# A gated-attention kernel's load phase: where extra V rows go, where row norms run, and in which order the output weights load

## The chip, the cores and the metric

The kernel runs on one core of one Trainium2 chip. The metric is the device time of one execution in microseconds (us). Before the change the median of three runs is 871.95 us (871.49 to 874.51). The engines are named as in the profile: PE (TensorE, matmul) with PEld (its weight loads), DVE (VectorE), ACT (ScalarE), POOL (GpSimd) and SP (SyncE, which here only issues DMAs).

## The reference, cut to what matters

Two blocks in sequence, in bf16. Block A is a recurrent attention: the 2048 rows are cut into 64 segments of 32; each segment is preceded by 8 memory rows, and the first 8 output rows of a segment are the memory of the next. Block B is a gated MLP with a spatial mixing matrix.

```python
for s in range(n_seg):                     # 64 segments, one after the other
    h = concatenate([mem, xs])             # 8 + 32 rows, D = 512
    q, k, v = h @ Wq, h @ Wk, h @ Wv       # 32 heads of 128
    p = softmax(mask(q @ k.T * scale))
    o = (p @ v) @ Wo
    mem = o[:8]; outs.append(o[8:])
h  = x + A(layernorm(x)); h2 = h + B(layernorm(h))
```

The weights Wq, Wk, Wv and Wo are 4 MB each.

## The kernel before

All instructions are put out by one Python function, `fast_path`, in an order written by hand; an `Emitter` derives the semaphore waits from tokens that each operation reads and writes. On each engine the instructions run in the order in which they are emitted. There is no planner; DMAs are issued by SP in order (function `sp`), and a few by ACT and POOL.

**Tiling of block A.** A segment has 40 rows: 8 of memory and 32 of x. The first 24 rows of x and the memory make up a tile of 32 columns (`hT`), which is worked on segment by segment. The last 8 rows of each segment, the "extra rows", do not depend on the memory; they are worked on for 16 segments at once (a chunk, 16 x 8 = 128 rows, `hTe`). Chunk `ck` gives queries and keys of the extra rows (`qkx_mm`, L410, into `QTx` in SBUF) and values (`vx_mm`, L429). One call of `qkx_mm` or `vx_mm` fills one PSUM bank with 16 matmuls; it is called a group here. A chunk has 16 Q/K groups and 8 V groups (`n` from 0 to 7: half `b = n // 4`, quarter `c = n % 4`).

The V groups come out with a row per extra row and 4 heads in a line, and attention wants 8 extra rows of one segment times 16 groups of heads on the partitions. So `vx_evac` copies a group to SBUF (L441, L443) and stores it to the DRAM tensor `vext_d` (L449), and `load_vx(s)` reads the rows of segment `s` back into `Vx` (L457). For chunk 0 the evacuated groups lie in `part`; the store is split: the rows of segments 0 and 1 go first, on the queue of ACT or POOL, the other rows on SP's.

**The load phase.** SP issues two tiles of x, Wq in four quarters, three tiles of x, the initial memory, then Wk, Wv and Wo in four quarters each (Wo by heads 0 to 7, 8 to 15 and so on). Meanwhile:

- Rows of x are normalized in place (`ln_inplace` = `ln_stats`, L357 and L358 on DVE, L359 and L361 on POOL, then `ln_apply`, L367 on DVE) and transposed by PE (`xT`, L375). Tiles 0 and 1 are the extra rows of chunks 0 and 1 and are normalized and transposed first; tiles 4, 5 and 6 are normalized in one stretch after the eighth step of the loop below.
- The constants for mask, sums and selections (`late_consts`) are made on POOL right behind these three norms.
- A loop of 16 steps works through the 16 Q/K groups of chunk 0 and, in each second step, one of chunk 1. `start_group` gives each group the next of four PSUM banks (`ebank`) and evacuates it on ACT and DVE in turn (L419, L421).

**A segment** (loop over `s`): Q and K (`QK`, L480), scores (`S_half`, L518 and L524), V (`V_half`, L571), sums (L539, L544), P times V (`PV_half`, L588; L594 for the extra rows, which reads `Vx`), the output projection (`Wo`, L621, in two halves of the columns, heads in the quarters 0, 2, 1, 3), its evacuation (`part_evac`, L636, L638) and the new memory rows (`mem_out`, L645, copied by L650), which the next segment's Q and K wait for. Into the gaps go groups of later chunks: one whole group per segment (`gx`, bank `XB`) and "atoms" of four matmuls (`gv`, `pour`, bank `VXB`). Segment 0 also does the eight V groups of chunk 0 (`start_v`) and two Q/K groups of chunk 1, between its own steps.

Block B follows after the last segment.

## Time and profile before

| | |
|---|---|
| median of 3 runs | 871.95 us (871.49 to 874.51) |
| the profiled execution | 872.18 us, span 870.4 us |
| PE busy | 846.9 us, 97% of the span, 20941 matmuls |
| DVE busy | 527.5 us, 61% |
| ACT busy | 420.9 us, 48% |
| POOL busy | 161.6 us, 19% |
| DMA | 76.29 MB; 20.48 MB of them in the first 85 us |
| mean granted TensorE clock | 0.995 of full speed |

The span is what the profile covers from the first to the last instruction; the execution's own time is 1.8 us longer. A line of the timeline gives the start, the length, the engine, the source line, the operation, output and inputs, and in square brackets the idle time of the engine before it and who ended that. A matmul that is pipelined behind another is shown with its drain, so lengths of neighbours overlap a little. A tile is named as in the program with f_ in front. Line numbers (L410) are those of the kernel before.

### The profile page before, as it was taken

The numbers are of one execution on the slowest core, as the hardware profiler recorded it, in microseconds if no ns is written. First come the engines' busy times: TensorE is split into PE (matmuls) and PEld (weight loads), VectorE is DVE, ScalarE is ACT, GpSimd is POOL, SyncE is SP. The second block draws the span as 40 slices with busy tenths as digits, with TensorE's granted clock in tenths as the row PEclk, the third lists the DMA queues.
The fourth block names the chain that finished last, engine by engine and source line by source line (L and its number), as shares of the span: only waits on it lengthen the run. The fifth ranks groups of instructions, "written<-read, shape, count | busy, mean of one in ns | idle before, by whom it ended". The sixth has DMA issues, their size and how long they took to land.

```text
span 870.4 us, 45576 instructions
## 1 busy us (share of the span) xinstructions
PE 846.9 (97%) x20941; PEld 474.5 (55%) x20941; DVE 527.5 (61%) x1192; ACT 420.9 (48%) x1083; POOL 161.6 (19%) x408
## 2 busy tenths in 40 slices
PE   6889999999999999999999999999999999999997
PEld 6645555555555655555565655455555544444443
DVE  3456667666666666666666666566666558363443
ACT  2345555555555555555555555455655566400000
POOL 1421212111211211121212121212211114100000
PEclk9999999999999999999999999999999999999999
DMA  9962223122230310211212121423322299132101
GB/s 324 377 189 63 65 55 65 44 61 65 61 56 26 86 46 25 73 46 53 61 42 53 46 61 43 108 67 89 70 68 62 61 224 337 35 104 91 50 13 38
DMA packets 109207, 76.29 MB, mean 88 GB/s; under 512 B 64104, under 2 KB 94512, under 8 KB 109008
## 3 DMA queue, kind: packets, MB, share of 16 engines
q1 hardware_dynamic: 108496, 73.04, 29.9%
q8 instruction: 166, 2.72, 1.3%
q14 instruction: 33, 0.27, 0.1%
q0 software_dynamic: 192, 0.20, 0.1%
q10 hardware_dynamic: 320, 0.07, 0.0%
HBM read 41.75 MB, written 20.91 MB: 72 GB/s over the span
## 4 chain that ended last, share of the span: by engine, by line
PE 95%; DVE 1%; DMA 1%; issue 1%; ACT 1%; POOL 1%; DVEq 0%; POOLq 0%
PE f_ps L480 26%; PE f_ps L621 15%; PE f_ps L571 12%; PE f_ps L1098 11%; PE f_ps L410 7%; PE f_ps L672 4%; PE f_ps L429 3%; PE f_ps L1091 3%; PE f_ps L1192 3%; PE f_ps L588 2%; PE f_ps L518 2%; PE f_ps L731 2%; PE f_ps L539 1%; PE f_ps L594 1%; PE f_ps L645 1%; PE f_ps L1059 1%
## 5 line engine op out<-in xcount | busy, mean ns | idle before, releaser
L480 PE MATMUL f_ps<-f_arena,f_hT 128*32 128x512 bf16 x4096 | 240.4, 380 | 0.1
L487 ACT ACTIVATE f_Tst<-f_ps 128x512 bf16<-128x512 f32 x256 | 145.9, 596 | 77.5 <-PE f_ps L480 77.5
L480 PEld LDWEIGHTS f_ps<-f_arena,f_hT 128*32 128x32 bf16 x4096 | 93.0, 96 | 103.4 <-ACT f_hT L650 32.7
L621 PE MATMUL f_ps<-f_arena,f_cT 128*32 128x256 bf16 x4096 | 130.8, 275 | 3.6 <-ACT f_cT L607 2.2
L571 PE MATMUL f_ps<-f_arena,f_hT 128*32 128x512 bf16 x2048 | 132.8, 378 | 0.0
L621 PEld LDWEIGHTS f_ps<-f_arena,f_cT 128*32 128x32 bf16 x4096 | 99.2, 97 | 36.7 <-ACT f_cT L607 31.6
L493 DVE STREAM_TRANSPOSE f_QT<-f_Tst 128x256 uint32<-128x256 uint32 x128 | 57.1, 446 | 82.2 <-ACT f_Tst L487 82.2
L580 DVE CAST f_V_sb<-f_ps 128x512 bf16<-128x512 f32 x128 | 88.4, 691 | 29.5 <-PE f_ps L571 29.5
L1098 PE MATMUL f_ps<-f_arena 128*128 128x512 bf16 x448 | 99.6, 379 | 0.1
L503 POOL COPY f_QT<-f_arena 128x256 bf16<-128x256 bf16 x64 | 30.6, 478 | 296.9 <-PE f_ps L524 296.9
L607 ACT ACTIVATE f_cT<-f_ps 128x320 bf16<-128x320 f32 x128 | 49.0, 434 | 59.2 <-PE f_ps L594 59.2
L609 DVE TENSOR_SCALAR f_cT<-f_ps 128x320 bf16<-128x320 f32 x128 | 56.9, 487 | 31.3 <-PE f_ps L594 31.3
L1098 PEld LDWEIGHTS f_ps<-f_arena 128*128 128x128 bf16 x448 | 43.7, 98 | 53.0 <-issue 0.6
L410 PE MATMUL f_ps<-f_hTe,f_arena 128*128 128x128 bf16 x1024 | 67.9, 225 | 3.8 <-DVE f_arena L421 3.2
L638 DVE CAST f_part<-f_ps 128x256 bf16<-128x256 f32 x64 | 27.2, 425 | 69.0 <-PE f_ps L621 69.0
L410 PEld LDWEIGHTS f_ps<-f_hTe,f_arena 128*128 128x128 bf16 x1024 | 60.3, 101 | 13.2 <-issue 8.5
L496 DVE STREAM_TRANSPOSE f_KT<-f_Tst 128x256 uint32<-128x256 uint32 x128 | 55.4, 433 | 8.1
L571 PEld LDWEIGHTS f_ps<-f_arena,f_hT 128*32 128x32 bf16 x2048 | 44.5, 95 | 28.9 <-issue 0.4
L551 ACT ACTIVATE f_R_sb<-f_ps 128x160 f32<-128x160 f32 x128 | 39.0, 305 | 42.6 <-PE f_ps L544 42.6
L1104 DVE TENSOR_TENSOR f_arena<-f_ps,f_arena 128x512 f32<-128x512 f32 x28 | 19.3, 690 | 60.7 <-PE f_ps L1098 60.7
L650 ACT ACTIVATE f_hT<-f_ps 128x16 bf16<-128x16 f32 x126 | 23.2, 184 | 55.8 <-PE f_ps L645 55.3
L636 ACT ACTIVATE f_part<-f_ps 128x256 bf16<-128x256 f32 x64 | 24.6, 384 | 46.5 <-PE f_ps L621 46.5
(113 smaller groups left out, 1123.1 us busy)
## 6 DMA issues: line engine op xcount, KB each, us to landing
wT_d<-f_wst SPq DMA_DIRECT2D x32, 256.0 KB, 2.2
f_arena<-wT_d SPq DMA_DIRECT2D x32, 256.0 KB, 5.2
f_arena<-in_A_Wq_dram SPq DMA_DIRECT2D x4, 1024.0 KB, 8.7
f_arena<-in_A_Wk_dram SPq DMA_DIRECT2D x4, 1024.0 KB, 14.0
f_arena<-in_A_Wv_dram SPq DMA_DIRECT2D x4, 1024.0 KB, 14.6
f_arena<-in_A_Wo_dram SPq DMA_DIRECT2D x4, 1024.0 KB, 13.6
f_Vx<-vext_d SPq DMA_DIRECT2D x62, 64.0 KB, 2.7
vext_d<-f_Vs SPq DMA_DIRECT2D x24, 128.0 KB, 2.1
```

Of the source, the lines that this page charges most:

```text
L410: pe(lambda e, h=h, dc=dc, hh=hh: e.matmul(ps[:, bank, hh * 128:(hh + 1) * 128], lhsT=ws[:, dc, h * DH:(h + 1) * DH], rhs=hTe[:, ck % 3, d ...
L480: pe(lambda e, dc=dc, c=c, rhs=rhs: e.matmul(ps[32 * c:32 * c + 32, bank, :], lhsT=hT[:, sl, dc, :], rhs=rhs, start=(dc == 0), stop=(dc == ...
L487: act(lambda e: e.activation(out=Tst[:, tb, :].rearrange("p (hp i r) -> p hp i r", i=32, r=2), in_=ps[:, bank, :].rearrange("p (hp r i) -> ...
L493: dve(lambda e: e.transpose(out=dst, in_=src), reads=[("T", tb)], writes=[("QT", b)])
L496: dve(lambda e: e.transpose(out=dst, in_=src), reads=[("T", tb)], writes=[("KT", b)])
L551: act(lambda e: e.activation(out=R_sb[:, b, :], in_=ps[:, bank, 224:384], func=ACT.Ln, scale=LNS), reads=[PB(bank)], writes=[("R", b)])
L571: pe(lambda e, dc=dc, c=c, c0=c0: e.matmul(ps[32 * c:32 * c + 32, bank, :], lhsT=hT[:, sl, dc, :], rhs=w_v[:, dc, c0:c0 + 512], start=(dc ...
L580: dve(lambda e: e.tensor_copy(out=V_sb[:, b, :], in_=ps[:, bank, :]), reads=[PB(bank)], writes=[("V", b)])
L607: act(lambda e: e.activation(out=dst, in_=src, func=ACT.Copy, scale=UNSC), reads=[PB(PVB[c])], writes=[("cT", c)])
L609: dve(lambda e: e.tensor_scalar(out=dst, in0=src, scalar1=UNSC, scalar2=None, op0=ALU.mult), reads=[PB(PVB[c])], writes=[("cT", c)])
L621: pe(lambda e, h=h, g=g, i=i, b=b, c=c: e.matmul(ps[32 * g:32 * g + 32, bank, 0:d1 - d0], lhsT=cTh[:, i, 8:40], rhs=w_o[:, h, d0:d1], star ...
L1098: pe(lambda e: e.matmul(ps[:, bank, 0:TB], lhsT=z2[:, sc, fb * 128:(fb + 1) * 128], rhs=wTb[tb % 2][:, :, sc, :], start=(n == 0), stop=(n ...
```

## The change

Four things change, all around the load phase and the first segments.

1. **Extra V rows.** `vext_d` gets another layout, so that a group's store writes 1 KB rows (4 heads in a line) instead of rows of 256 bytes; the load of a segment's rows reads pieces of 256 bytes instead of 512. Stores are not split any more and all go through SP. Segment 0's `Vx` doesn't go through DRAM: `vx_first` picks its 8 rows out of the eight evacuated groups by 32 matmuls with a shifted identity (`Z_sb`, made on POOL by two more operations) and one evacuation on ACT. Group 0 of chunk 0 lies in `xo` instead of `part`, as `part` slot 0 is written at the end of segment 0.
2. **Norms and constants.** `late_consts` is emitted right after the first two norms. Tile 1 is transposed after two groups. Tiles 4, 5 and 6 get their statistics and their application in the steps 6 to 9 of the loop, a piece per step.
3. **Wo.** It is loaded in eight pieces, in the order in which `Wo` uses the quarters (0, 2, 1, 3). Segment 0 does the first three quarters for both column halves before the last quarter.
4. **Order in segment 0.** V groups 2 and 3 follow the scores of the second half, 4 to 7 follow the sums; three banks instead of four are in turn. V group 0 of chunk 1 stands in four pieces around the output projection. No atoms are poured in segment 0, two instead of one in segments 1 to 3; over the whole kernel their number is the same, so that one atom fewer is left for segment 44.

```diff
@@ -235,6 +235,7 @@
     ones = sb("ones", [128, 128], BF)
     onesrc = sb("onesrc", [128, 160], BF)
     G_sb = sb("G_sb", [128, M], BF)
+    Z_sb = sb("Z_sb", [128, 56], BF)
     F_sb = sb("F_sb", [128, 32], BF)
     Sc = sb("Sc", [128, 128], BF)
     m0 = sb("m0", [M, D], BF)
...
-    vext_d = nc.dram_tensor("vext_d", [NCK, 16, 128, 2 * DH], BF, kind="Internal").ap()
+    vext_d = nc.dram_tensor("vext_d", [NCK, 128, 2, 16, DH], BF, kind="Internal").ap()
     xn2_d = nc.dram_tensor("xn2_d", [RB, 128, D], BF, kind="Internal").ap()
     h_d = nc.dram_tensor("h_d", [RB, 128, D], BF, kind="Internal").ap()
     NP = 10
@@ -317,10 +318,13 @@
     pool(lambda e: e.affine_select(out=ident[:], in_=onesrc[:, 0:128], pattern=[[-1, 128]], compare_op=ALU.is_equal,
                                    fill=0.0, base=0, channel_multiplier=1), reads=["onesrc"], writes=["ident"])
     pool(lambda e: e.memset(mhalf[:], -0.5), writes=["mhalf"])
-    em.mark_const("ident", "mhalf", "mask", "ones", "G", "F", "Sc", "bsp")
+    em.mark_const("ident", "mhalf", "mask", "ones", "G", "F", "Sc", "bsp", "Z")
 
     def late_consts():
         pool(lambda e: e.memset(ones[:], 0.0), writes=["ones"])
+        pool(lambda e: e.affine_select(out=Z_sb[:, :], in_=onesrc[:, 0:56], pattern=[[-1, 56]], compare_op=ALU.is_equal,
+                                       fill=0.0, base=24, channel_multiplier=1), reads=["onesrc"], writes=["Z"])
+        pool(lambda e: e.memset(Z_sb[:, 32:56], 0.0), writes=["Z"])
         pool(lambda e: e.memset(Sc[:], 0.0), writes=["Sc"])
         pool(lambda e: e.memset(mask[:], 0.0), writes=["mask"])
         for c in range(4):
@@ -430,9 +434,9 @@
                                                        start=(dc == 0), stop=(dc == DC - 1), tile_position=(0, 32 * c)),
                    reads=[("hTe", ck % 3), ("W", 2, n // 2)], writes=[PB(bank)])
 
-    def vx_evac(ck, n, bank, eng="act", queue="sp"):
+    def vx_evac(ck, n, bank, eng="act"):
         if ck == 0:
-            t, tok = part[:, n, :], [("part", n, 0), ("part", n, 1)]
+            t, tok = vx_home(n)
         else:
             j = vcnt[0] % 2
             vcnt[0] += 1
@@ -442,20 +446,31 @@
         else:
             dve(lambda e: e.tensor_copy(out=t, in_=ps[:, bank, :]), reads=[PB(bank)], writes=tok)
         b, c = n // 4, n % 4
-        dst = vext_d[ck, 4 * c:4 * c + 4, :, b * DH:(b + 1) * DH].rearrange("g t e -> t g e")
-
-        for k, (i0, i1) in enumerate(((0, 2), (2, CK)) if ck == 0 else ((0, CK),)):
-            r = slice(8 * i0, 8 * i1)
-            em.add("sp" if k else queue, lambda e, r=r: e.dma_start(dst[r], t[r].rearrange("p (g e) -> p g e", g=4)), dma=True,
-                   reads=tok, writes=[("vext", ck, n, k)])
+        sp(lambda e: e.dma_start(vext_d[ck, :, b, 4 * c:4 * c + 4, :], t.rearrange("p (g e) -> p g e", g=4)),
+           reads=tok, writes=[("vext", ck, n)])
 
     vcnt = [0]
 
-    def load_vx(s, queue="sp"):
+    def vx_home(n):
+        return (part[:, n, :], [("part", n, 0), ("part", n, 1)]) if n else (xo[:, 0, :], [("xo", 0)])
+
+    def vx_first(bank):
+        for g in range(4):
+            for b in range(2):
+                for c in range(4):
+                    t, tok = vx_home(4 * b + c)
+                    pe(lambda e, g=g, b=b, c=c, t=t: e.matmul(
+                        ps[32 * c:32 * c + 32, bank, b * DH:(b + 1) * DH], lhsT=Z_sb[:, 24 - 8 * g:56 - 8 * g], rhs=t[:, g * DH:(g + 1) * DH],
+                        start=(g == 0), stop=(g == 3), skip_group_check=True, tile_position=(0, 32 * c)),
+                        reads=tok + ["Z"], writes=[PB(bank)])
+        act(lambda e: e.activation(out=Vx[:, 0, :, :].rearrange("p b e -> p (b e)"), in_=ps[:, bank, 0:2 * DH], func=ACT.Copy),
+            reads=[PB(bank)], writes=[("Vx", 0)])
+
+    def load_vx(s):
         i = s % CK
-        assert all(("vext", s // CK, n, 0) in em.last_w for n in range(8))
-        em.add(queue, lambda e: e.dma_start(Vx[:, s % NVX, :, :], vext_d[s // CK, :, 8 * i:8 * i + 8, :]), dma=True,
-               reads=[("vext", s // CK, n, k) for n in range(8) for k in range(2 if 2 <= s < CK else 1)], writes=[("Vx", s % NVX)])
+        assert all(("vext", s // CK, n) in em.last_w for n in range(8))
+        sp(lambda e: e.dma_start(Vx[:, s % NVX, :, :], vext_d[s // CK, 8 * i:8 * i + 8, :, :, :].rearrange("t b g e -> g t b e")),
+           reads=[("vext", s // CK, n) for n in range(8)], writes=[("Vx", s % NVX)])
 
 
     QKB = {(0, 0): 0, (0, 1): 1, (1, 0): 6, (1, 1): 7}
@@ -621,7 +636,7 @@
                 pe(lambda e, h=h, g=g, i=i, b=b, c=c: e.matmul(
                     ps[32 * g:32 * g + 32, bank, 0:d1 - d0], lhsT=cTh[:, i, 8:40], rhs=w_o[:, h, d0:d1], start=(c == 0 and b == 0),
                     stop=(c == 3 and b == 1), tile_position=(0, 32 * g)),
-                    reads=[("cT", c), ("Wo", h // 8)], writes=[PB(bank)])
+                    reads=[("cT", c), ("Wo", b, c)], writes=[PB(bank)])
 
     def cTx_copy(s):
         j = s % 4
@@ -671,7 +686,7 @@
             h = 16 * b + 4 * qr + g
             pe(lambda e, h=h, g=g, i=8 * qr + bg: e.matmul(ps[32 * g:32 * g + 32, WXB, :], lhsT=cTx[:, rb % 2, i, :], rhs=w_o[:, h, :],
                                                            start=(i < 4), stop=(i >= H - 4), tile_position=(0, 32 * g)),
-               reads=[("cTx", rb % 2), ("Wo", h // 8)], writes=[PB(WXB)])
+               reads=[("cTx", rb % 2), ("Wo", b, qr)], writes=[PB(WXB)])
 
     def WoX_evac(rb):
         act(lambda e: e.activation(out=partx[:], in_=ps[:, WXB, :], func=ACT.Copy), reads=[PB(WXB)], writes=["partx"])
@@ -755,7 +770,7 @@
     def pour():
         if s > 3 * CK and not gv.atoms and zx and s + 2 < NSEG:
             z2_atoms()
-        return gv.pour(1)
+        return gv.pour(2 if 0 < s < 4 else 0 if s == 0 else 1)
 
     NWT = S // 64
 
@@ -767,23 +782,21 @@
     act(lambda e: e.preload_act_table_set("natural_log_exp_and_others"))
     for j in range(2):
         ln_inplace(j)
-        xT(j, 6 + j)
-        xe_copy(j, 6 + j)
+    late_consts()
+    xT(0, 6)
+    xe_copy(0, 6)
     for hq in range(4):
         load_w(1, hq)
-    ebank = (2, 3, 4, 5)
+    ebank = [2, 3, 4, 5]
     scnt = [0]
 
     def start_group(mm, ev, *a):
         cnt = scnt[0]
         scnt[0] += 1
-        bk = ebank[cnt % 4]
+        bk = ebank[cnt % len(ebank)]
         mm(*a, bk)
         eng = "act" if cnt % 2 == 0 else "dve"
-        if mm is vx_mm:
-            ev(*a, bk, eng, {"act": "act", "dve": "pool"}[eng])
-        else:
-            ev(*a, bk, eng)
+        ev(*a, bk, eng)
 
     def start_x(ck, i):
         start_group(qkx_mm, qkx_evac, ck, i)
@@ -793,12 +806,15 @@
 
     for i in range(16):
         start_x(0, i)
+        if i == 1:
+            xT(1, 7)
+            xe_copy(1, 7)
         if i % 2 == 1:
             start_x(1, i // 2)
-        if i == 7:
-            for j in range(4, 7):
-                ln_inplace(j)
-            late_consts()
+        if 7 <= i < 10:
+            ln_apply(i - 3)
+        if 6 <= i < 9:
+            ln_stats(i - 2)
         if i == 10:
             xT(4, 6)
             ring_copy(0, 6)
@@ -812,9 +828,11 @@
     for hq in range(4):
         load_w(2, hq)
     wor = A_Wo.rearrange("h e d -> e h d")
-    for hq in range(4):
-        sp(lambda e, hq=hq: e.dma_start(w_o[:, 8 * hq:8 * hq + 8, :], wor[:, 8 * hq:8 * hq + 8, :]), writes=[("Wo", hq)])
-        em.mark_const(("Wo", hq))
+    for c in (0, 2, 1, 3):
+        for b in range(2):
+            h0 = 16 * b + 4 * c
+            sp(lambda e, h0=h0: e.dma_start(w_o[:, h0:h0 + 4, :], wor[:, h0:h0 + 4, :]), writes=[("Wo", b, c)])
+            em.mark_const(("Wo", b, c))
 
 
     class Gap:
@@ -853,7 +871,7 @@
         mms = [lambda ck=ck, n=n, dc=dc: vx_mm(ck, n, VXB, dc) for dc in range(DC)]
         gv.add(VXB, mms, lambda: vx_evac(ck, n, VXB, "act"))
 
-    for n in range(8):
+    for n in range(1, 8):
         vx_group(1, n)
     for ck, i0 in ((1, 10), (2, 0), (3, 0)):
         if ck == 2:
@@ -919,13 +937,11 @@
             if mi == 0:
                 mask_put(1)
         if s == 0:
+            ebank[:] = [3, 4, 5]
             for n in range(2):
                 start_v(n)
         S_half(s, 0)
         sm_exp(0)
-        if s == 0:
-            for n in range(2, 4):
-                start_v(n)
         V_half(s, 0)
         V_evac(0, "dve")
         if s > 0:
@@ -937,7 +953,7 @@
         sm_exp(1)
         sm_rcp(0)
         if s == 0:
-            for n in range(4, 8):
+            for n in range(2, 4):
                 start_v(n)
         V_half(s, 1, (1, 2, 3) if s > 0 else range(DC))
         lastop["v"] = em.by_eng["pe"][-1]
@@ -955,12 +971,15 @@
         V_evac(1, "dve")
         sm_norm(1, dve)
         if s == 0:
-            for j in range(2):
-                load_vx(j, "pool")
-            for i in range(8, 10):
-                start_x(1, i)
+            for n in range(4, 8):
+                start_v(n)
+            load_vx(1)
+            start_x(1, 8)
+            vx_first(ebank[scnt[0] % 3])
+            scnt[0] += 1
+            start_x(1, 9)
         late = pour()
-        ev = [gx.pop(0)()] if gx else [z2_group()] if zx and s > 3 * CK else []
+        ev = [] if s == 0 else [gx.pop(0)()] if gx else [z2_group()] if zx and s > 3 * CK else []
         PV_half(s, 0)
         PV_half(s, 1)
         cT_evac(0, "act")
@@ -977,13 +996,27 @@
             for f in late:
                 f()
             late = []
-        Wo((0, 2, 1, 3), OB, 0, OC)
-        part_evac(s, 0)
-        Wo((0, 2, 1), OB2, OC, D)
-        if s + 1 < NSEG:
+        if s == 0:
+            vx_mm(1, 0, XB, 0)
+            Wo((0, 2, 1), OB, 0, OC)
+            Wo((0, 2, 1), OB2, OC, D)
+            Wo((3,), OB, 0, OC)
+            part_evac(s, 0)
+            Wo((3,), OB2, OC, D)
+            part_evac(s, 1)
+            vx_mm(1, 0, XB, 1)
+            vx_mm(1, 0, XB, 2)
             mem_out(s, 0)
-        Wo((3,), OB2, OC, D)
-        part_evac(s, 1)
+            vx_mm(1, 0, XB, 3)
+            vx_evac(1, 0, XB, "act")
+        else:
+            Wo((0, 2, 1, 3), OB, 0, OC)
+            part_evac(s, 0)
+            Wo((0, 2, 1), OB2, OC, D)
+            if s + 1 < NSEG:
+                mem_out(s, 0)
+            Wo((3,), OB2, OC, D)
+            part_evac(s, 1)
         cTx_copy(s)
         if j4 == 3 and rb > 0:
             WoX_scatter(rb - 1, XB, True)
```

## The prediction

> **What bounds the kernel now.** I read the page first, then the busy time by stretches, TensorE's waits, the timeline of the first 70 us, and the landings of the loads.
>
> ```profile
> PE 846.9 (97%) x20941; PEld 474.5 (55%) x20941; DVE 527.5 (61%) x1192; ACT 420.9 (48%) x1083; POOL 161.6 (19%) x408
> PE   6889999999999999999999999999999999999997
> DMA  9962223122230310211212121423322299132101
> ```
>
> TensorE is busy 97% of the span: from the third slice on, every slice but the last has nine tenths. The change can win only where TensorE stands still, in the first slices (21.8 us each), and there the DMA row has 9 9 6. So two things can end this stage, TensorE's own order and the load of the weights. By stretches (us, then busy time of PE, PEld, DVE, ACT, POOL, granted clock, DMA share, GB/s):
>
> ```profile
> 9.00:25.00 16.00, 16.00 (x274) 15.79 (x272) 6.13 (x11) 5.12 (x10) 0.90 (x3) 1.00 1.06 383
> 25.00:30.00 5.00, 1.84 (x25) 1.67 (x24) 2.81 (x6) 1.08 (x2) 2.95 (x11) 0.89 1.04 385
> 30.00:38.00 8.00, 8.00 (x142) 7.49 (x139) 2.08 (x3) 2.86 (x6) 5.42 (x25) 0.86 1.05 384
> 42.00:46.00 4.00, 4.00 (x100) 2.02 (x96) 2.05 (x4) 1.88 (x4) 0.75 (x1) 1.00 1.10 348
> 54.00:57.50 3.50, 1.65 (x60) 0.73 (x56) 0.88 (x3) 0.48 (x2) 1.09 (x2) 1.00 0.43 106
> ```
>
> There are two holes in TensorE, at 25 to 30 and at 54 to 57.5. The DMA engines are full until about 50 us: 383 to 385 GB/s up to 38 us, some 350 while Wo comes. TensorE's waits in the first 85 us name the causes:
>
> ```profile
> PE f_ps L410 <- DVE f_arena L421: 3.2, 1, 3.2
> PE f_ps L594 <- DMA f_Vx<-vext_d: 0.8, 1, 0.8
> PE f_ps L410 <- DVE f_V_sb L580: 0.7, 1, 0.7
> ```
>
> The first hole in the timeline (start, length, work):
>
> ```profile
> 6.99 0.57 POOL L361 TENSOR_TENSOR f_rs<-f_rs,f_mhalf 128x1 f32<-128x1 f32 x1
> 21.68 0.69 DVE L357 BATCH_NORM_STATS2 f_st<-f_part 128x6 f32<-128x512 bf16 x1
> 28.03 0.41 DVE L367 TENSOR_SCALAR f_part<-f_part,f_mv,f_rs 128x512 bf16<-128x512 bf16 x1 [1.00 <-POOL f_rs L361]
> 28.05 0.20 POOL L323 MEMSET f_ones<- 128x128 bf16 x1
> 28.36 1.28 DVE L421 CAST f_arena<-f_ps 128x512 bf16<-128x512 f32 x2
> 29.10 3.48 PE L410 MATMUL f_ps<-f_hTe,f_arena 128*128 128x128 bf16 x32 [3.16 <-DVE f_arena L421]
> 32.50 0.41 PE L375 MATMUL f_ps<-f_ident,f_part 128*32 128x128 bf16 x16
> 32.84 2.85 PE L410 MATMUL f_ps<-f_hTe,f_arena 128*128 128x128 bf16 x48
> 36.15 1.96 PE L410 MATMUL f_ps<-f_hTe,f_arena 128*128 128x128 bf16 x32
> 38.04 3.64 PE L480 MATMUL f_ps<-f_arena,f_hT 128*32 128x512 bf16 x64
> 39.00 0.23 POOL L346 TENSOR_SCALAR_AFFINE_SELECT f_mask<-f_mask 32x32 bf16<-32x32 bf16 x1
> ```
>
> VectorE does three row norms in one piece, 21.68 to 28.44, and evacuates nothing meanwhile; TensorE fills its four banks and stops for 3.16 us. The next 32 matmuls take 3.48 us where 32 take 1.96 us at 36.15: the clock had dropped (0.89 and 0.86 in the stretches) and cost another 1.5 us. The shorter idle at 54 to 57.5, 1.85 of 3.5 us, left the clock at 1.00. Below, segment s begins with its Q matmuls (L480): segment 0 at 38.04 us.
>
> **The change, part by part.** When the loads land decides how much of the holes comes back: the first K quarter is needed by the ninth Q/K group of chunk 0, the last Wo quarter at the end of segment 0 (first and last start of the issue, then time to landing):
>
> ```profile
> L303 SPq DMA_DIRECT2D f_arena<-in_A_Wk_dram x1: 400/400/400, 9.2 to 9.2; - x1
> DMA to landing us min/median/max: 11.5/11.5/11.5
> ...
> L816 SPq DMA_DIRECT2D f_arena<-in_A_Wo_dram x1: 2841/2841/2841, 39.9 to 39.9; - x1
> DMA to landing us min/median/max: 11.7/11.7/11.7
> ```
>
> The first K quarter is there at 20.7, the last Wo quarter at 51.6. SyncE issues everything up to Wo in the same order as before and waits for no engine; Wo comes in eight issues of half the size, the same bytes in the same rows. I keep both times.
>
> *Start and norms.* The first Q group now goes ahead of the second row transpose, which brings it forward by less than 1 us. That gain is lost at the K weights: 12 groups come before them; VectorE's evacuation (0.69) of the last of these ended at 21.68, so its matmuls ended near 20.9; moved forward by less than 1 us they end near 20 and TensorE waits some 0.7 us. From 20.7, 12 groups remain (8 of chunk 0, 4 of chunk 1): three take 2.79 us (32.84 to the next row transpose at 35.63), so 11.2; three row transposes of 0.34 (32.50 to 32.84) 1.0; the memory transpose 0.2. Segment 0 then begins at 20.7 + 12.4 = 33.1 instead of 38.04. This needs the spread norms to stop nobody: each puts 0.69 + 0.41 us and a small aggregate on VectorE per group and a half (1.4 us), beside some 0.65 for each second evacuation, so VectorE falls behind by about 1 us and four banks (3.6 us) cover it. The constants move ahead of these norms on GpSimd: 28.05 to 39.23 is 11.2 us, two operations for Z add 0.4 (a memset 0.2, a select 0.23 by the rows above), so from 7.6 (the end of L361, the second norm's rstd) they run to 19.2. The first late norm's statistics come at about 19; its rstd is at most some 0.5 us late, hidden by the banks. With that cover gone it is the first rival.
>
> *Segment 0.* Its pieces (L429 is V of the extra rows, L571 V of the segment):
>
> ```profile
> 43.36 1.90 PE L429 MATMUL f_ps<-f_arena,f_hTe 128*32 128x512 bf16 x32
> 45.09 1.03 PE L571 MATMUL f_ps<-f_arena,f_hT 128*32 128x512 bf16 x16
> 57.51 1.71 PE L621 MATMUL f_ps<-f_arena,f_cT 128*32 128x256 bf16 x56 [0.56 <-ACT f_cT L607]
> 58.62 0.38 ACT L636 ACTIVATE f_part<-f_ps 128x256 bf16<-128x256 f32 x1 [0.83 <-PE f_ps L621]
> 59.58 0.62 PE L480 MATMUL f_ps<-f_arena,f_hT 128*32 128x512 bf16 x8
> 66.60 0.27 PE L588 MATMUL f_ps<-f_E_sb,f_V_sb 32*128 32x40 bf16 x16
> 67.61 1.71 PE L621 MATMUL f_ps<-f_arena,f_cT 128*32 128x256 bf16 x56 [0.54 <-ACT f_cT L607]
> 69.68 0.61 PE L480 MATMUL f_ps<-f_arena,f_hT 128*32 128x512 bf16 x8
> ```
>
> The new order on TensorE up to the last Wo quarter: Q and K 3.5 (the row of 3.64 less its last drain); eight V groups, 1.73 a pair (43.36 to 45.09), 7.0; two V halves 1.9; scores and sums about 0.6 (an estimate from the gaps between these rows); two K groups 1.9 (the row at 36.15 above); the 32 selecting matmuls for Vx, same shape as the 16 row-transpose matmuls of 0.41, 0.8; P·V with its evacuation 1.0 (66.60 to 67.61); 48 of the Wo matmuls 1.71 x 48/56 = 1.5. Sum 18.2, so TensorE asks for the last Wo quarter at 33.1 + 18.2 = 51.3 and gets it at 51.6: work and load meet. The 20 matmuls of the next V group that stood before P·V at s = 0 are gone or fill the gaps behind Wo. Three banks instead of four: a group of 0.9 us returns to its bank after two others, 1.8 us, against an evacuation of 0.6 to 0.7 and its handshake, so no wait. Then the last quarter for both halves, evacuation, mem_out and its copy: 0.96 from L636 to L480 (58.62 to 59.58) behind about 0.5 of matmuls: 1.5. Segment 1 begins at 53.1 instead of 59.58: 6.5 us.
>
> *Vx.* Eight small stores leave the queues of ScalarE and GpSimd, and two loads GpSimd's; neither engine was late there, so this counts nothing. SyncE gets one load more. The round trip through DRAM ahead of segment 0 (0.8 of waiting, and what stands before it) goes. What is late next is the load for segment 1: it waits on SyncE behind all eight stores, and the store of V(1,0), the load for segment 2 and the first spatial-weight piece queue behind it; nobody needs those for 10 us. Rows for it:
>
> ```profile
> L449 SPq DMA_DIRECT2D vext_d<-f_part x1: 493/493/493, 53.6 to 53.6; - x1
> DMA to landing us min/median/max: 2.1/2.1/2.1
> ...
> f_Vx<-vext_d SPq DMA_DIRECT2D x62, 64.0 KB, 2.7
> vext_d<-f_Vs SPq DMA_DIRECT2D x24, 128.0 KB, 2.1
> ```
>
> The stores (then 256-byte pieces) had landed by 55.7; with 1 KB pieces and the same queue I take 55. A Vx load now moves 256 pieces of 256 bytes instead of 128 of 512. It is bounded by the store of 512 pieces of 256 bytes, 2.1, and its own 2.7; I take 2.7, the same operation, and land at 58. Segment 1 needs it 7.0 us after its start (59.58 to 66.60), at 60.1. Later loads run more than a segment ahead and cost nothing; if a segment ran dry of that cover each would cost its excess over some 17 us.
>
> [...]
>
> *Atoms.* Segments 1 to 3 each carry four more L429 matmuls, segment 44 four fewer: 1.73/32 each, 12 cost 0.65 and 4 return 0.2. Net 0.45.
>
> Sum: 6.5 - 0.45 = 6.0 us. The profiled execution (872.18, span 870.4) becomes 866.2; the median of the runs, 871.95, becomes 866.0.
>
> **Rivals.** *Norms still stop TensorE.* If the constants run 5 us longer beside VectorE's work, the first rstd comes at 24, VectorE holds the evacuations again, and the 3.16 + 1.5 us return: segment 0 at 37.8, segment 1 at 57.8, 1.8 - 0.45 gained: 870.6. This is "the change doesn't do what it says". For it: the overlap is new. Against it: GpSimd's rows of 0.2 to 0.3 us were taken while VectorE evacuated too.
>
> *Segment 0 is TensorE's, not the load's.* Ten groups in three banks and evacuations that share ScalarE with exp and ln: if each waits 0.3, 3 us are added less the 0.3 of slack: 868.7. For it: the one wait of 0.7 of L410 for VectorE's V evacuation, in this very stage. The other way, if Wo comes at the earlier 383 GB/s (4.19 MB in 10.9 instead of 12.0 us), TensorE ends first and 0.3 more is won, 865.7; with the shorter matmul counts 864.9.
>
> *The Vx load for segment 1 is late*, the case on the other side: each us beyond 60.1 costs one, beyond 66.1 the kernel is slower, beyond 70.5 by half a per cent; a landing at 72 would give 866.0 + 11.9 = 877.9. For it: one queue, in order, behind 4 MB of Wo. Against it: from Wo's 51.6 on, stores and load would have to take 19 us where the rows above give 6.4.
>
> **How the numbers follow.** A half per cent, 4.4 us, is about what a measurement of this kernel can tell from no change. The forecast, 864.9 to 867.5: 0.66. Segment 0 bound by TensorE, 867.5 to 869.5: 0.20, of which a quarter still passes the half per cent. Norms: 0.09. Vx late: 0.05, nearly all of it slower. Faster 0.71, same 0.25, slower 0.04. The range leaves out the last two and a little below: 864.7 to 869.4; both signs do not share the chance, so no second range.
>
> [...]
>
> **What would show it.** Right: no L410 wait on DVE near 26 us and clock 1.00 from 25 to 38; L480 first at 33; the L621 matmuls waiting under 1 us for Wo's DMA near 51; segment 1 at 53; no L594 wait on DMA; later segments 10.1 us apart as before (59.58 to 69.68). Wrong: a DVE hole of 3 us, gaps before L429, or L594 waiting in segment 1.

## The result, and the profile after

In ten runs of each on one chip the changed kernel took 869.2 us (median, 866.81 to 870.65) and the kernel before 872.89: a ratio of 0.9955, 95% interval 0.9938 to 0.9971. That is 3.7 us less, 0.45%: by the median inside the half per cent that the forecast took as its border (it gave 0.25 to that and 0.71 to more), with an interval that reaches to both sides of it. The forecast of 866.0 is 3.2 us too low; the range (864.7 to 869.4) holds the time just below its upper end. Of the 3.2, 0.9 is the kernel before, which took 872.89 here and not the 871.95 that the forecast started from; the gain is 3.7 us where 6.0 was forecast. The profiled execution took 869.43 us, with a span of 867.6, against 872.18 and 870.4. New lines are numbered by the changed kernel: Q/K groups L414 (L410 before), V groups L433 (L429), Q of a segment L495 (L480), P·V of the extra rows L609 (L594), output projection L636 (L621), selecting matmuls L462.

The changed kernel's page: span, busy times, and the DMA queue that brings instructions (packets, MB, share of the DMA engines' time).

```profile
span 867.6 us, 45627 instructions
...
PE 846.3 (98%) x20966; PEld 478.3 (55%) x20973; DVE 526.2 (61%) x1190; ACT 422.3 (49%) x1086; POOL 159.0 (18%) x404
...
q8 instruction: 166, 2.72, 1.3%
```

Its busy times by stretches (columns as for the kernel before):

```profile
25.00:30.00 5.00, 5.00 (x108) 4.47 (x106) 3.55 (x7) 2.33 (x5) 1.26 (x3) 1.00 1.05 387
30.00:38.00 8.00, 8.00 (x158) 5.82 (x159) 3.45 (x7) 3.64 (x8) 0.00 (x0) 1.00 1.05 386
...
50.00:54.00 4.00, 2.37 (x80) 1.89 (x69) 0.89 (x2) 1.20 (x3) 0.40 (x1) 0.78 0.90 306
54.00:57.50 3.50, 3.41 (x80) 2.15 (x72) 1.21 (x3) 1.31 (x4) 0.22 (x1) 0.76 0.13 34
```

The hole at 25 to 30 us is gone and the clock there is 1.00. A new hole stands at 50 to 54, and behind it the clock is 0.76, where before it was 1.00. TensorE's waits in the first 85 us:

```profile
PE f_ps L379 <- DVE f_xn L371: 5.9, 1, 5.9
PE f_ps L414 <- DMA f_arena<-in_A_Wq_dram: 2.1, 1, 2.1
PE f_ps L636 <- issue: 1.6, 1, 1.6
PE f_ps L636 <- ACT f_cT L622: 1.1, 2, 0.5
PE f_ps L414 <- ACT f_hTe L395: 0.7, 1, 0.7
```

The waits for VectorE's evacuation and for `Vx` have gone. New are 0.7 us for the copy of tile 1's transpose, and 1.6 us ahead of the output projection that nothing in the profile ends ("issue": no semaphore, no transfer). TensorE's timeline at these places:

```profile
8.58 3.22 PE L414 MATMUL f_ps<-f_hTe,f_arena 128*128 128x128 bf16 x32 [2.08 <-DMA f_arena<-in_A_Wq_dram]
11.73 0.41 PE L379 MATMUL f_ps<-f_ident,f_xn 128*32 128x128 bf16 x16
12.84 12.68 PE L414 MATMUL f_ps<-f_hTe,f_arena 128*128 128x128 bf16 x224 [0.70 <-ACT f_hTe L395]
...
34.23 2.13 PE L495 MATMUL f_ps<-f_arena,f_hT 128*32 128x512 bf16 x36
...
52.27 3.57 PE L636 MATMUL f_ps<-f_arena,f_cT 128*32 128x256 bf16 x64 [1.63 <-issue]
56.62 0.62 PE L495 MATMUL f_ps<-f_arena,f_hT 128*32 128x512 bf16 x8
```

Segment 0 begins at 34.23 instead of 38.04, segment 1 at 56.62 instead of 59.58: 2.96 us of the 6.5 forecast. From segment 1 to the end of the span it is 811.0 us (867.6 less 56.62), before 810.8.

### The profile page after: what moved, and what is told of

It reads as the page before. It is cut to its first block, busy times and chain, and to the rows that moved or that the text cites. A ratio compares the mean times of both kernels' runs of the same rounds, so it can differ in the third digit from the quotient of the medians.

```text
span 867.6 us, 45627 instructions
## 1 busy us (share of the span) xinstructions
PE 846.3 (98%) x20966; PEld 478.3 (55%) x20973; DVE 526.2 (61%) x1190; ACT 422.3 (49%) x1086; POOL 159.0 (18%) x404
## 3 DMA queue, kind: packets, MB, share of 16 engines
q1 hardware_dynamic: 104992, 73.24, 30.4%
## 4 chain that ended last, share of the span: by engine, by line
PE 95%; DVE 2%; issue 1%; DMA 1%; ACT 1%; POOL 0%; SPq 0%; DVEq 0%; POOLq 0%
PE f_ps L495 26%; PE f_ps L636 14%; PE f_ps L586 13%; PE f_ps L1131 11%; PE f_ps L414 7%; PE f_ps L687 4%; PE f_ps L433 3%; PE f_ps L1225 3%; PE f_ps L603 2%; PE f_ps L533 2%; PE f_ps L1124 2%; PE f_ps L746 2%; PE f_ps L554 1%; DVE f_st L1106 1%; PE f_ps L660 1%
## 5 line engine op out<-in xcount | busy, mean ns | idle before, releaser
L495 PE MATMUL f_ps<-f_arena,f_hT 128*32 128x512 bf16 x4096 | 241.0, 380 | 0.8 <-issue 0.4
L495 PEld LDWEIGHTS f_ps<-f_arena,f_hT 128*32 128x32 bf16 x4096 | 95.2, 96 | 103.0 <-ACT f_hT L665 33.0
L636 PE MATMUL f_ps<-f_arena,f_cT 128*32 128x256 bf16 x4096 | 130.1, 275 | 3.3 <-ACT f_cT L622 1.6
L636 PEld LDWEIGHTS f_ps<-f_arena,f_cT 128*32 128x32 bf16 x4096 | 99.3, 97 | 35.2 <-ACT f_cT L622 30.9
L414 PE MATMUL f_ps<-f_hTe,f_arena 128*128 128x128 bf16 x1024 | 66.4, 222 | 2.8 <-DMA f_arena<-in_A_Wq_dram 2.1
L414 PEld LDWEIGHTS f_ps<-f_hTe,f_arena 128*128 128x128 bf16 x1024 | 58.6, 99 | 12.7 <-issue 11.1
L586 PEld LDWEIGHTS f_ps<-f_arena,f_hT 128*32 128x32 bf16 x2048 | 45.9, 95 | 27.2
```

The lines of the kernel that those rows point to most:

```text
L414: pe(lambda e, h=h, dc=dc, hh=hh: e.matmul(ps[:, bank, hh * 128:(hh + 1) * 128], lhsT=ws[:, dc, h * DH:(h + 1) * DH], rhs=hTe[:, ck % 3, d ...
L495: pe(lambda e, dc=dc, c=c, rhs=rhs: e.matmul(ps[32 * c:32 * c + 32, bank, :], lhsT=hT[:, sl, dc, :], rhs=rhs, start=(dc == 0), stop=(dc == ...
L586: pe(lambda e, dc=dc, c=c, c0=c0: e.matmul(ps[32 * c:32 * c + 32, bank, :], lhsT=hT[:, sl, dc, :], rhs=w_v[:, dc, c0:c0 + 512], start=(dc ...
L636: pe(lambda e, h=h, g=g, i=i, b=b, c=c: e.matmul(ps[32 * g:32 * g + 32, bank, 0:d1 - d0], lhsT=cTh[:, i, 8:40], rhs=w_o[:, h, d0:d1], star ...
```

## The experiments

All times below are read from one profiled execution of each kernel; "half rate until" is the moment from which matmuls of 128 columns follow each other by 0.056 us instead of 0.107. The trace's records of the granted clock begin at that moment (at 11.29 in the changed kernel, 16.52 when it ran again, 4.70 with the warm start); the stretches ahead of it show 1.00 because no record stands there. Times and ratios are against the kernel before on the same chip, with 95% intervals.

| kernel | half rate until | segment 0 | segment 1 | 0 to 1 | 1 to end | median us | ratio |
|---|---|---|---|---|---|---|---|
| before | 11.9 | 38.04 | 59.58 | 21.54 | 810.8 | 872.89 | |
| changed | 11.3 | 34.23 | 56.62 | 22.39 | 811.0 | 869.2 | 0.9955 (0.9938 to 0.9971) |
| changed, again | 16.6 | 35.98 | 55.97 | 19.99 | 810.8 | 868.61 | 0.9942 (0.9923 to 0.9961) |
| tile 1 first | 12.8 | 33.76 | 54.62 | 20.86 | 809.2 | 867.81 | 0.9936 (0.9913 to 0.9958) |
| 64 instructions more | 17.1 | 36.45 | 56.64 | 20.19 | 811.0 | 867.63 | 0.9944 (0.9923 to 0.9965) |
| half of Wo | 16.9 | 36.84 | 55.86 | 19.02 | 811.5 | 867.81 | 0.9942 (0.9922 to 0.9961) |
| norms alone | 13.4 | 34.08 | 60.29 | 26.21 | 809.9 | 872.69 | 0.9999 (0.9979 to 1.0019) |
| norms as before | 11.6 to 12.6 | 39.80 | 59.36 | 19.56 | 809.0 | 870.17 | 0.9964 (0.9944 to 0.9984) |
| warm start | 4.7 | 33.42 | 55.63 | 22.21 | 810.6 | 866.63 | 0.9922 (0.9900 to 0.9944) |
| warm, fewer | 7.2 | 33.26 | 55.31 | 22.05 | 808.6 | 865.73 | 0.9931 (0.9917 to 0.9945) |
| Wo turned round | 11.3 | 33.70 | 56.57 | 22.87 | 809.7 | 867.02 | 0.9934 (0.9918 to 0.9951) |

The runs of one kernel scatter by 2 to 4 us either way, and "1 to end" differs by up to 3 us from kernel to kernel, so the columns of the load phase tell the variants apart, and the medians only where they differ by more.

### What stands ahead of the output projection: the kernel again, tile 1 first, a shift, half of Wo

Four kernels on one chip. The changed kernel unaltered:

> The changed kernel, unaltered, once more. Its first profile has TensorE idle for 1.35 us between the first weight load and the first matmul of segment 0's output projection (50.92 to 52.27), then half clock for 3.4 us. Theory 1 (refill): TensorE waits for its next block of 256 instructions, which comes through the same DMA engines as the weights; the wait stands before the same instruction again (number 1728 in TensorE's order), between 0.5 and 2 us, and segment 1 begins between 55.5 and 57. Rival 2 (data): it waited for a quarter of Wo whose landing the trace does not show; the wait ends when Wo's last pieces land, near 52. Rival 3 (chance): a single event of that execution; without it segment 1 begins near 53.6. Time: about 0.9955 of the kernel before by 1 and 2.

Tile 1 transposed ahead of the first Q group, as before the change:

```diff
-    xT(0, 6)
-    xe_copy(0, 6)
+    for j in range(2):
+        xT(j, 6 + j)
+        xe_copy(j, 6 + j)
...
-        if i == 1:
-            xT(1, 7)
-            xe_copy(1, 7)
```

> The changed kernel with tile 1 transposed ahead of the first Q group, as before the change. In the changed kernel the second transpose and its copy stand behind two groups at half clock and cost TensorE a wait of 0.70 us; the first group started at 8.58 in both kernels because Wq landed only then. I expect the 13th group at 21.0 instead of 21.8 and segment 0 at 33.4 instead of 34.23. Theory 1 (refill): the pace of the refills, some 6 us per 256 instructions while weights load, sets the rest of the stage, so the 0.8 us is kept and segment 1 begins near 55.8. Rival 2 (Wo's landing sets the end): segment 1 stays at 56.6. Time against the kernel before: 0.9945 by 1, 0.9955 by 2.

64 TensorE instructions more at the start (32 matmuls and their weight loads), in time that TensorE stands idle:

```diff
+    for k in range(32):
+        c = k % 4
+        pe(lambda e, c=c: e.matmul(ps[32 * c:32 * c + 32, 5, 0:128], lhsT=ident[:, 32 * c:32 * c + 32], rhs=ident[:, :], ...
```

> The changed kernel with 32 more small matmuls (64 instructions with their weight loads) right behind the first transpose, where TensorE is idle for 2.1 us; their result is overwritten. Theory 1 (refill): the borders of TensorE's blocks of 256 instructions move 64 instructions forward in the program, so the waits without a cause move: one of 1 to 1.5 us in the V groups of segment 0 (near 43.8) and at most 0.5 us in P times V, none at the first matmul of the output projection; whether the clock falls depends on where the idle lies. Rival 2 (data): the wait stays before the first matmul of the output projection and ends near 52. Time against the kernel before: 0.992 to 0.996 by 1, 0.9955 by 2. The small matmuls may also warm the clock for the first two groups, up to 0.7 us at segment 0, by either.

Half of Wo not loaded:

```diff
-            sp(lambda e, h0=h0: e.dma_start(w_o[:, h0:h0 + 4, :], wor[:, h0:h0 + 4, :]), writes=[("Wo", b, c)])
+            if c % 2 == 0:
+                sp(lambda e, h0=h0: e.dma_start(w_o[:, h0:h0 + 4, :], wor[:, h0:h0 + 4, :]), writes=[("Wo", b, c)])
+            else:
+                pool(lambda e, h0=h0: e.memset(w_o[:, h0:h0 + 4, :], 0.0), writes=[("Wo", b, c)])
```

> The changed kernel with quarters 1 and 3 of Wo (2 of 4 MB) left out of the load; GpSimd clears them instead, so half of the output projection is multiplied by zeros. The DMA engines are free some 6 us earlier. Theory 1 (refill): refills come faster from about 46 us on, the wait before the output projection goes, the clock stays full, and segment 1 begins between 52.5 and 53.5, 3 to 4 us earlier than in the changed kernel; time 0.991 of the kernel before. Rival 3 (the order of work in segment 0 alone, or the low density of matmuls, lowers the clock): the wait may go but the half clock stays, segment 1 near 55. By rival 2 the wait goes as well.

The first output-projection matmuls in the timelines of the four, in this order, and between the second and third the place to which the wait went in the shifted kernel. First, the kernel again:

```profile
53.26 1.93 PE L636 MATMUL f_ps<-f_arena,f_cT 128*32 128x256 bf16 x64 [0.53 <-ACT f_cT L622]
```

Tile 1 first:

```profile
51.91 1.93 PE L636 MATMUL f_ps<-f_arena,f_cT 128*32 128x256 bf16 x64 [1.90 <-issue]
```

Shifted by 64 instructions:

```profile
47.26 2.99 PE L433 MATMUL f_ps<-f_arena,f_hTe 128*32 128x512 bf16 x51 [0.67 <-issue]
53.92 1.93 PE L636 MATMUL f_ps<-f_arena,f_cT 128*32 128x256 bf16 x64 [0.22 <-ACT f_cT L622]
```

Half of Wo:

```profile
53.15 1.93 PE L636 MATMUL f_ps<-f_arena,f_cT 128*32 128x256 bf16 x64 [0.28 <-ACT f_cT L622]
```

The wait does not belong to the output projection's data: the quarter of Wo that the projection reads first had landed by 43.8 us in the changed kernel. In the shifted kernel no such wait is left ahead of the projection, and one of 0.67 stands in the V groups. The shift alone does not prove that the wait moved with the instructions, because segment 0 also began later there (36.45): the unaltered kernel, with segment 0 at 35.98, has only 0.53 ahead of the projection (0.28 is usual for the copy of `cT`) and 0.34 in the V groups.

What settles it is the place. Counted by TensorE's records (weight loads, matmuls and the few waits of its sequencer) from the first, the wait stands at the same kind of place each time: at records 1472, 1728 or 1984, that is 192 beyond a multiple of 256. The eleven traces hold 57 waits in which TensorE, at full clock up to then and with no semaphore to wait for, lets over 0.4 us pass from one start to the next; all 57, early or late in the kernel, stand at such a border. The page above has 166 packets on the instruction queue, all of 16 KB, and 41,939 records of PE and PEld: one packet for each 253. So, by these two counts, TensorE's program arrives in blocks of 256 instructions over the DMA engines that also bring the weights (1.3% of the time of the 16 engines went to that queue, 30.4% to the data's). The packets start at (read from the traces' DMA records, us):

```text
changed          23.86 30.80 37.13 43.66 49.67 53.51
tile 1 first     23.39 30.18 36.49 43.02 49.42 53.15
half of Wo       26.45 32.98 39.67 44.21 47.77 54.27
warm start       27.49 33.83 40.34 47.08 52.11 55.68
warm, fewer      29.99 36.18 42.78 49.37 53.74 57.21
```

Where TensorE waited at both ends of a block while the weights came, the step from packet to packet was 6.0 to 6.7 us (43.66 to 49.67 in the changed kernel, 43.02 to 49.42 with tile 1 first, 40.34 to 47.08 with the warm start, 42.78 to 49.37 with fewer instructions). Behind these, as the loads end, the steps in the four rows are 3.5 to 5.0. With half of Wo the two steps after 39.67 are 4.5 and 3.6, no such wait is left in segment 0, and 0 to 1 is the shortest of all, 19.02. A segment of 10.1 us with its 590 or so records uses a block in 4.4 us. TensorE resumes some 2.5 us after the packet's start (49.67 and 52.27; 49.42 and 51.91).

The expectations were right about the places and missed most sizes. In the kernel again, 0.5 to 2 us were expected before the same instruction, and 0.25 came beyond the copy. With tile 1 first, segment 1 began at 54.62 instead of 55.8, as the clock did not fall. The shift's wait was 0.67 near 47 us instead of 1 to 1.5 near 44. With half of Wo, segment 1 was expected at 52.5 to 53.5 and began at 55.86, because segment 0 began 2.6 us later than in the first profile of the changed kernel.

That half of Wo was multiplied by zeros changes nothing in the time of the matmuls (1.93 in both kinds of kernel). While GpSimd cleared the missing half, VectorE's last late norm application took 1.97 us (otherwise 0.41) and TensorE waited 0.69 us for an evacuation, which is part of the late segment 0 there.

### Which part pays: norms alone, norms undone, Wo turned round

Norms and constants put into the kernel before, and nothing else:

```diff
+    late_consts()
...
-        if i == 7:
-            for j in range(4, 7):
-                ln_inplace(j)
-            late_consts()
+        if 7 <= i < 10:
+            ln_apply(i - 3)
+        if 6 <= i < 9:
+            ln_stats(i - 2)
```

> The kernel before with one part of the change alone: the row norms of tiles 4 to 6 spread over three group pairs and the constants made early; extra V rows, their loads, the output weights and the order of segment 0 stay as before. Theory 1 (the norms are most of the gain, and the rest of the change gives little because segment 0 gets back what the refill and half speed take): no wait of TensorE on VectorE near 26 us, segment 0 at 33.4 to 33.9 (38.04 less 3.16 of idle, less 1.2 to 1.5 of half speed), segment 0 to segment 1 in 21.5 us as before, segment 1 at 55.2, span 866.0, some 868 us. Theory 2 (the round trip of the extra V rows through DRAM has no cover once segment 0 comes 4.5 us earlier, since its stores then run beside the load of the output weights): P.V of segment 0 waits for the extra V rows by 2 to 4.5 us instead of 0.8, segment 0 to 1 takes 23.5 to 26 us, segment 1 at 57 to 59.6, span 868 to 870.4.

The changed kernel with the same lines turned back:

> The changed kernel with the norms of tiles 4 to 6 again in one piece and the constants late; all else is as in the changed kernel. Theory 1: VectorE again evacuates nothing for some 7 us, TensorE stops for about 3 us near 26 and runs at half speed after it, segment 0 at 37 to 38; by then the output weights are early (51.6, asked for at 55), so segment 0 to 1 takes 18.5 to 20 us, segment 1 at 56 to 58, span 867 to 869, 869 to 871 us: a good half of what the whole change gains, or nothing, is left. Theory 2 (the selection by matmuls and the new order of segment 0 give nothing by themselves): segment 0 to 1 in 21.5 us as before, segment 1 at 59 to 59.6, span 870.

The changed kernel with Wo's loads in another order:

```diff
-    for c in (0, 2, 1, 3):
+    for c in (2, 1, 3, 0):
```

> The changed kernel with the third part turned round: the quarter of the output weights that is loaded last is the one that segment 0's output projection uses first (loads in the order 2, 1, 3, 0; use 0, 2, 1, 3 as before). Theory 1 (TensorE reaches the output projection at 50 to 52, later than the forecast had it relative to the load, or stands at a border anyway; the last quarter lands at 51.1 and 52.4): a wait of the first output-projection matmul on the load of 0.2 to 1.5 us, segment 1 at most 1 us later than with the changed kernel for the same start of segment 0: segment 0 to 1 in 20 to 22.5 us, and the time within 1 us of the changed kernel's, some 869. Theory 2 (using the last quarter last is what lets segment 0 end with the load): the wait is 2 us or more, segment 0 to 1 takes 23 us or more, some 871.

Norms alone, timeline of TensorE and its stretch behind:

```profile
55.48 0.24 PE L594 MATMUL f_ps<-f_E_sb,f_Vx 32*128 32x64 bf16 x4 [3.61 <-DMA f_Vx<-vext_d]
56.42 3.18 PE L621 MATMUL f_ps<-f_arena,f_cT 128*32 128x256 bf16 x56 [0.51 <-ACT f_cT L607]
```
```profile
54.00:57.50 3.50, 1.51 (x48) 1.09 (x52) 1.49 (x3) 0.77 (x2) 0.40 (x1) 0.55 0.39 97
```

Norms as before, timeline:

```profile
29.73 3.60 PE L414 MATMUL f_ps<-f_hTe,f_arena 128*128 128x128 bf16 x32 [3.13 <-DVE f_arena L425]
56.64 1.93 PE L636 MATMUL f_ps<-f_arena,f_cT 128*32 128x256 bf16 x64 [0.28 <-ACT f_cT L622]
```

Wo turned round, timeline:

```profile
52.21 3.58 PE L636 MATMUL f_ps<-f_arena,f_cT 128*32 128x256 bf16 x64 [2.05 <-issue]
```

Norms alone bring segment 0 forward by 3.96 us, as much as the whole change does, and all of it is lost: the stores and loads of the extra V rows now run beside Wo and bring `Vx` only 1.1 us earlier than before, P·V waits 3.61 us for it instead of 0.8, the clock falls to half for 6.8 us (the 56 matmuls take 3.18 instead of 1.71), and segment 1 begins at 60.29, later than before and 0.7 beyond Theory 2's own range, which had no fall of the clock in it. The measured ratio is 0.9999. So the norms gain nothing without the rest: Theory 2 holds.

Conversely, with the norms undone the hole of 3.1 us comes back in segment 0's way (39.80) and segment 1 begins at 59.36: in its load phase this kernel gains 0.2 us of the changed kernel's 3.0. Its median is nevertheless below the kernel before by 0.36%, with an interval that leaves out no change; its span saves 2.0 us, of which 1.8 lie after segment 1, where the two kernels differ only by some atoms and the layout of the `Vx` loads. What moves there was not settled. In segment 0 Theory 1 was right (19.56, within its 18.5 to 20, where Theory 2 had 21.5), so the rest of the change does save 2.0 us there, with segment 0 beginning 1.8 us later than before. But this kernel missed Theory 1's numbers for its start (37 to 38): the half rate behind the hole lasted 6.8 us instead of 3.4.

The order of Wo's quarters is worth nothing visible: turned round, TensorE passes the wait for the first piece of the last-loaded quarter at 50.44 and stands at the same border (record 1728) until 52.21, with the same fall of the clock; the second piece landed at 51.34, within that time, so the border hides it. 0 to 1 is 22.87 against 22.39, a little over Theory 1's 20 to 22.5 and below the 23 of Theory 2, and the time is not longer.

### The start: TensorE warm, and with fewer instructions

Tile 1 first, and TensorE's idle time before its first real work filled, in the second kernel with matmuls of 512 columns of a tile of ones made that wide:

```diff
+    def warm(n):
+        for k in range(n):
+            pe(lambda e: e.matmul(ps[:, 5, 0:128], lhsT=ident[:, :], rhs=ident[:, :], start=True, stop=True, ...
+    warm(40)
     for j in range(2):
         xT(j, 6 + j)
         xe_copy(j, 6 + j)
+        if j == 0:
+            warm(24)
```

> The changed kernel with tile 1 transposed ahead of the first Q group, as in the kernel before, and with 64 matmuls of the identity with itself added to TensorE's idle time at the start (40 ahead of tile 0's transposes, 24 behind them); their results are not used. Theory 1 (TensorE starts at half rate, a matmul of 128 columns each 0.107 us instead of 0.056, and becomes full only after some 3 to 5 us without a hole; the start is then bounded by the first K quarter): full rate from about 6 us, the first Q group at 8.6 at 0.056 a matmul, 12 groups done near 19.5 to 20, a wait of about 1 us for the first K quarter (lands near 20.7), segment 0 at 33.1 against 33.76 with tile 1 first alone and 34.23 to 35.98 with the changed kernel. Theory 2 (the half rate at the start comes from something else than idle, such as the full load on the DMA engines or a fixed time since the launch): the first Q groups run at 0.107 us a matmul until 12 to 13 us as before, segment 0 at 33.8 to 34.3. Either way the border at instruction 1472 or 1728 of TensorE moves 128 instructions earlier in the program, and a causeless wait of 0.5 to 1.7 us stands there in segment 0 (V groups); segment 1 at 53.5 to 55, span 863 to 865, some 866.5 us.

> As the warm start, but the same idle time is filled by 16 matmuls of 512 columns instead of 64 of 128 (the constant tile of ones is made 512 columns wide for it; their results are not used): 96 TensorE instructions fewer ahead of segment 0, nothing else. Theory 1 (while the weights come in, blocks of 256 TensorE instructions are supplied at one per 6.4 us or so, and TensorE stands still at a border whenever it got there sooner): segment 0 at 33.4 as with the warm start, with the wait of 0.8 for the first K quarter; the borders 1472 and 1728 are met 96 instructions later in the program, 1984 not before segment 1; the causeless waits of segment 0 sum to 0.8 to 2 us instead of 3.2, segment 0 to 1 takes 20 to 21 us instead of 22.21, segment 1 at 53.4 to 54.5. Theory 2 (the waits belong to places in the work, the selecting matmuls and the output projection, and not to the count of instructions): they stand again at the selecting matmuls and in the output projection and sum to 3 us, segment 1 at 55.5. Span 863.5 to 865 under theory 1, 866 under theory 2.

Warm start, timeline:

```profile
20.92 3.91 PE L414 MATMUL f_ps<-f_hTe,f_arena 128*128 128x128 bf16 x64 [0.83 <-DMA f_arena<-in_A_Wk_dram]
...
42.99 0.83 PE L586 MATMUL f_ps<-f_arena,f_hT 128*32 128x512 bf16 x11 [0.83 <-issue]
49.73 0.24 PE L462 MATMUL f_ps<-f_part,f_Z_sb 128*32 128x128 bf16 x3 [0.81 <-issue]
...
54.59 0.27 PE L636 MATMUL f_ps<-f_arena,f_cT 128*32 128x256 bf16 x1 [0.68 <-issue]
```

Warm with fewer instructions, timeline:

```profile
20.93 3.73 PE L414 MATMUL f_ps<-f_hTe,f_arena 128*128 128x128 bf16 x64 [0.77 <-DMA f_arena<-in_A_Wk_dram]
45.20 2.12 PE L433 MATMUL f_ps<-f_arena,f_hTe 128*32 128x512 bf16 x35 [0.94 <-issue]
51.82 0.22 PE L603 MATMUL f_ps<-f_E_sb,f_V_sb 32*128 32x40 bf16 x7 [1.62 <-issue]
```

Theory 1 holds for the start. Filled with work from 1.4 us on, TensorE ran at half rate until 4.7 in the first kernel (3.3 us of work) and until 7.2 in the second (5.8), and then it waited for the first K quarter (0.83 and 0.77) as the forecast had it. But what was won there did not arrive at segment 1: it begins at 55.63 and 55.31, later than with tile 1 first alone (54.62), which fits borders that are met sooner. In the second kernel the waits moved to the V groups and P·V, away from the selecting matmuls and the output projection, as Theory 1 said of the places; its sizes missed: the waits sum to 2.56 us (0.94 and 1.62) instead of 0.8 to 2, no less than the 2.32 of the first, 0 to 1 takes 22.05 instead of 20 to 21, and 96 instructions fewer gained 0.3 us at segment 1. TensorE's count of instructions ahead matters less than the packets' pace: they start at 42.78 and 49.37, with tile 1 first at 43.02 and 49.42, although segment 0 began half a microsecond earlier.

The last kernel's 865.73 us is the lowest median of all. Its interval (0.9917 to 0.9945) just meets the changed kernel's (0.9938 to 0.9971), and most of its lead over the changed kernel's profile (3.7 us of span) lies after segment 1 (2.4), so it isn't shown to be the warm start's.

## Why the prediction was right in sign and 3 us short

*The norms: right.* The hole and the half speed behind it went, no evacuation was late, and the constants on GpSimd delayed nobody. The rival "norms still stop TensorE" fell.

*The start: K's landing as the bound, mis-sized by 1.1 us.* Forecast 33.1 for segment 0, measured 34.23. The step that failed is "forward by less than 1 us": the first Q group began at 8.58, as before (8.62), since it waited for Wq, and tile 1's transpose behind two groups cost a wait of 0.70 for its copy and 0.41 of its own, which before had filled the wait for Wq. So the 13th group began at 21.79, after K's quarter had landed (20.88), and that quarter set nothing. With tile 1 first segment 0 begins at 33.76. With TensorE warm, K does set it: 20.92 plus 12.5 is 33.42, where the forecast had 20.7 plus 12.4.

The forecast also missed the half rate at the start, which the tables of stretches don't show (1.00, for want of a record). In the changed kernel it ended at 11.3, ahead of the wait of 0.7. In three of the six profiles with that wait (the kernel again, the shift, half of Wo) it did not: the wait fell into TensorE's warm-up, half rate lasted to 16.6 to 17.1, and segment 0 began at 35.98 to 36.84. The same kernel thus gave 34.23 and 35.98.

*Segment 0: the work right, the end wrong by 2.4 us.* "Work and load meet", with the last Wo quarter asked for at 51.3 and there at 51.6, is the step that failed. The work up to there was as long as forecast: by its weight load's start TensorE was ready for the whole projection at 50.92 (34.23 and 16.7; the forecast had 33.1 and 18.2 less 1.5 for the matmuls of the projection). It then stood still for a block of its own program, until 52.27; from there on no matmul of the projection waited for a piece of Wo, so the load, whose last piece landed at 52.44, was not what ended segment 0. The forecast had no term for that; 1.63 less the usual 0.28 for the copy of `cT` is 1.35 us. Then the clock fell: 64 matmuls in 3.57 us, where the other kernels need 1.93, 1.64 more. The rest came out 0.6 shorter, which makes 2.4 (22.39 less the 20.0 of the forecast). Together with the start's 1.1, less 0.3 after segment 1, it is the 3.2 us by which the profiled execution is over its forecast of 866.2.

This split holds for one execution. In the second profile of the same kernel the clock did not fall and the wait was 0.53; 0 to 1 took 19.99 us, the forecast's 20.0, and the whole error at segment 1 lay in the start (35.98 against 33.1). What the forecast lacked in both is a term for TensorE's own state: its half rate at the start and the supply of its program.

The forecast's sum keeps two waits of TensorE, 0.7 and 0.3 us, and no fall of the clock behind them. The changed kernel could not show that, as neither came where it was meant; in the two warm kernels the wait for K did come (0.83 and 0.77) and the clock stayed: the 64 matmuls behind it took 3.91 and 3.73 us, 0.06 each. The wait that did come in the changed kernel, 1.63, was followed by a fall, and with tile 1 first one of 1.90 was not. The falls last 3.4 us (changed, Wo turned round) or 6.8 (norms alone, norms as before). In the records of the granted clock, up to the last one, a change lies a whole number of steps of 3.41 us behind the one before: 5, 1, 152, 1 and 92 steps in the kernel before (17.07, 3.41, 518.83, 3.41 and 314.03 us), 12, 1 and 238 in the changed one (40.96, 3.41 and 812.37).

Counted in these steps from the first record of the granted clock, the two waits differ: the 1.63 of the changed kernel lies in one step (48.83 to 52.25), and the 1.90 with tile 1 first is cut at 50.36, which leaves 1.55 in the second. Up to the last 15 us of the eleven traces, six steps at full clock with 1.61 us of idle or more were followed by half rate (2.96 and 1.71 in the kernel before, 1.61 in the changed one), and none with 1.55 or less; in the last 15 us two with 1.9 to 2.0 were not (2.0 in the changed kernel, 861.21 to 864.62), so idle time is not the whole rule.

*Vx: right.* P·V of no segment waited for it, and segments 1 to 3 take 10.32 us each, 4 and 5 10.1, by the four added matmuls (one atom) in each. The stores had landed by 55.43 and the load for segment 1 by 57.58; the forecast had 55 and 58. By the page after, the load of 256-byte pieces takes 2.8 us to land, against 2.7 with 512 bytes:

```profile
f_Vx<-vext_d SPq DMA_DIRECT2D x63, 64.0 KB, 2.8
```

The round trip through DRAM was counted with its 0.8 us; norms alone show that this was worth 3.6 us of waiting and the fall of the clock, once the norms were out of the way. The forecast never asked what the norms would gain without it.

*The rivals.* "Segment 0 is TensorE's, not the load's", 868.7, came nearest in time and in what it says, but by another mechanism: no group waited for its bank. The late `Vx` load, the case of the other side, did not come in the changed kernel; what it describes is what happened to norms alone.

## What to carry to other kernels

Ask of a stage in which the DMA engines are full not only when data land but when the instructions do: count the weight loads and matmuls, and look for waits without a semaphore at equal distances in that count (256 here). Two holes in a row hide each other: price an edit with the other one undone, since the second may take back all that the first gives (norms alone: 3.96 us at segment 0, a ratio of 0.9999). And do not put a wait for another engine into the time when TensorE still runs at half rate: a wait of 0.7 us some 4 us into its work went with some 4 us more of it in three of six profiles.

## What the runs showed of the hardware that was not expected

- TensorE's program comes in blocks of 256 instructions, by 16 KB packets on a DMA queue that carries nothing else, during the whole execution (166 in all, for 41,939 records). Where TensorE waited for them with the weights loading, a block took 6.0 to 6.7 us, some 40 instructions a microsecond; a segment later on uses some 58 (590 in 10.1 us). Waits at the borders were 0.3 to 2.05 us.
- Segment 1 began within 54.6 to 56.6 in all eight profiles of kernels that have both the spread norms and the selecting matmuls, while segment 0 began anywhere from 33.3 to 36.8. The supply of the program fits this where segment 0 began early; where it began late (the kernel again, half of Wo) few or no waits stand at a border, so there it is not shown to be the bound.
- The half rate at the start (0.107 us for a matmul of 128 columns) lasted from 8 us to between 11.3 and 17.1 (where work began at 1.4, to 4.7 and 7.2), and the page shows the granted clock as 1.00 there because its records begin only at the end of it. A wait of 0.7 us in it was followed by some 4 us more at half rate in three of six profiles.
- The records of the granted clock change in steps of 3.41 us (12 and 238 of them between the changes in the changed kernel), and a wait cost the clock where it lay in one such step (1.63 and 2.05 us) and not where it was cut in two (1.90).
- Why the stretch from segment 1 to the end varies between 808.6 and 811.5 us from kernel to kernel, with nearly the same work in it, is open. Some waits at borders and one fall of the clock near 551 us in the kernel before are part of it, but no run was made to separate them.
